# A new instruction plan for a fused retention and mixer kernel: first operations priced by their traced lengths, more zero products, a second bank for one turn

## The chip, the cores and the metric

The kernel runs on one core of a Trainium2 chip. The core has a matrix engine (TensorE, in the profile PE, its weight loads PEld), VectorE (DVE), ScalarE (ACT), GpSimd (POOL) and SyncE (SP), which issue their instructions each in program order and wait for one another through semaphores. POOL, SP and ACT also issue DMAs. The metric is the device time of one execution in microseconds (us), the median over runs.

## The reference

Four batches, eight heads, 768 tokens, head dimension 64, all inputs float32. First a retention layer, one state per head with its own decay, then a mixer block over tokens and channels:

```
for t in range(S):
    state = gamma[None, :, None, None] * state + np.einsum('bhd,bhe->bhde', k[:, :, t], v[:, :, t])
    y[:, :, t] = scale * np.einsum('bhd,bhde->bhe', q[:, :, t], state)
...
xt = x.transpose(0, 2, 1)
h = np.maximum(xt @ w_tok1, 0.0) @ w_tok2
u = x + h.transpose(0, 2, 1)
h2 = np.maximum(u @ w_ch1, 0.0) @ w_ch2
return (u + h2).astype(np.float32)
```

Here x is y with the heads side by side (512 channels); w_tok1 is 768 x 256, w_tok2 256 x 768, w_ch1 512 x 1536, w_ch2 1536 x 512.

## The kernel before

**Front** (L293 to L549), once per batch b and pair of heads p, so sixteen times. The 768 tokens are cut into six chunks of 128. In order of data:
- the loads of k, q and v (L270), issued by POOL as casting DMAs to float16, only the very first k (in the list HARD, L141) by SP in float32;
- the scaling of k by its decay, one step per head (`decayed`, L316), on VectorE or ScalarE; q is scaled either behind its turn, by one VectorE step (L356), or ahead of it (L316);
- the turn of k and of q (`turn`, L332): six or twelve TensorE transpositions into a bank of PSUM and a copy or scaling out of it (L361, L356), or, for batches 2 and 3, a transposing DMA issued by SP (L336). The list TURNS (L135) says which;
- k by v per chunk (L377), a chain of five prefix steps on VectorE (L387, L389), and its copy for both heads (L398, L401);
- the scores k by q (L417), four mask steps per pair on VectorE (L427), the products with v (L438) and with the prefix states (L447), the copy x (L453);
- the two token products (L467, L487) with a relu between (L476), the copies u and X (L493, L503), and the turn of u for the channel product (L533 and the copy L540, or a transposing DMA, L517).

**Back** (L551), once per batch: the wide product with w_ch1 (L571 for batches 0 and 1; L644, with seven products for eight, for batches 2 and 3), its relu (L587, L661, L682, L690), the narrow product with w_ch2, also with seven products for eight (L785, L795, with sums L749, copies L775 and additions L802), and the stores (L832), issued by SP or ACT. L875 and L888 make the sums of weights that the seven products need.

**What sets the order.** Front and back only make a list of 1,239 steps (`Op`, L22), each with one or more ways: an engine, an assumed cost in ns, and a function that emits its instructions. A planner, which isn't part of this file, has searched an order, an engine for each step and a bank of PSUM for each tile, from these costs; its answer is the string PLAN (L40), which `placed` (L72) decodes. In it two characters name a step, a digit the way where a step has several, a digit the bank where it opens one, and "+n" stands for n zero products: matmuls of a zero tile with 384 columns into a bank of their own (L906), which compute nothing of use. The main loop (L901) emits the steps in this order, so the string is the program order on every engine and in every DMA queue. The costs in the file have no other effect on the program.

A tile of k, q or v has four buffers; a load takes the one that came free first, and POOL, in order, holds all later loads while it waits for it. The first loads, which wait for none, follow each other in POOL's queue.

Of the kernel before, what the change touches and what calls it, by code (L numbers as in the profile page):

```python
# [9 lines left out]
F16 = mybir.dt.float16  # L10
# [11 lines left out]
class Op:  # L22
# [15 lines left out]
DIGITS = "0123456789abcdefghijklmnopqrstuvwxyzABCDEFGHIJKLMNOPQRSTUVWXYZ"  # L38

PLAN = (  # L40
    "0b07040f000d0c010g05021h1031i10e+d1n21j0060a1l41o1k009+12v61p1q1r0i1m0h082w1R02r1+11u412s10j+42t51s1x0l1v311S1"
    "0k1z1T02u01V11w1W1y1U0+21X024451Y0m1Z1t0261A11D31B1E+125421C020310272921+32x2283202y2z223352A356363402a42F500n"
    "2B0p0q+12d62I2C2301F00r0o2b2e2c02E252J2H+11G01H0s2G2D01I02N52O2K22L2f00z3f702M01J3i1K01M1L03j0u2g73701N1380v2h"
    "393a1O01P32P02i03H11Q00t2j2k02m3b3I3D13c2Q72l02R3E13n13e042n02S13d02p33h2T2W3F42U00y3g3k02X03l3o2V04f73m02o12q"
    "12Z33p00x3G12Y03004g3q64b13r3Q75240Aah34c13U3s03t3R0w0E3u03w3S3x0ae64J13z44d53v03B3T3A13J73C1ai3y03Y23K0B4K10C"
    "af3LaO4aP4e03M3NaR54L13O4h0ag4M14i3P1aj4jaSaQaU6aVaT4kaX3an43V54l3Z3WaoaWaYak63X04P1ap4004m410alaL40D42aM4314n"
    "14QamaC7aD19aI6aN4R47aEaJaZ0HaK1d44bf34501e4Sbgat44601aauaz7aAaw6axaB1caF5aGav4T0Iay5h14U4N7bhaH4o0164aq31bbi5"
    "4O4s5i0bjbkar0F4qb074pb345j1480as4rbob44ab14904W25034w65k04t1b51fbp0K4u4xb64b7b24v0bc7500G4Ybl3bd4V0bm4Z4z04y0"
    "bu5bq4X1516bn17b8bs3185425Q0be4A514524B0b97babvbt04C530bbbK0L4FbLbN4D05R0bw4E055570bz7bxbM4G0bO54H0bP15n65601g"
    "5W1bAby05o5p58bB5XbT5T05q5YbD5Z5905r5a6061bC05l05U05sbU05b05dbr0M5c05m5VbGbXbY0bEbH0J5u1047620bF5yca66r15e0c2c"  # L50
    "c75w5x6o0c6bV45S5t0bQ3c7cb04Icd5C0bW5D5f06p05v6s0c85gcf5z2cg05A5B0bR0S5E0c9bZcj6q5F7ck00P6tc0c3631354ce5GbSco6"
    "65H0bI1c165646u55I5J05Lch367cp6v5M0ci687695N06b46c5O16a0cl0O6d0c516wc410N5K15P16e66xcm6fcT2cs36y6g06zct6B05616"
    "D6Ccu6h0R6k6E6i0cUcN3cE56j06l1cVbJ1cFcv6cG6A16Fd526W1cwcO6G0cn7u0d25cP6m17v10Q6J1d3d46X0cQ36Kd6cRcx6Z1cSd77x16"
    "Hdb5dcdd7A47266I07Bcy3dw5cz700cr16ncH2d877C7y073cI7D0T74dxd9cAcJ756L1cW3cX76dydacK2cLdk7cM77dl7E7800V7FcZ6d06M"
    "5cYde2cB46Y6N0Wd1dfdmdq3dn6cCdr7G1dodgcDdp6O1dsdt5821dh7dC8A171dudv7zdidz6djdDdA8B1dG5dF8316S793724dEdBdY850dN"
    "6dH1dL7w7a7ddM00Y6P6Q06T06U07cdOe246R07be0dR8C8D0dP7H0173e31dSdQ0cq18617J7h67e27KdU7L8E07f7I7g00X7ie97eadZ7P37"
    "j07k10U7M07ldV7m07Qe17N107O07R1edee7n7q7S512dT8878G17o07p0847T7r1137U089dI2e7877V8H7s08I8a8J8b8KdJeo58cek8Le80"
    "8del7Yem8f71628F8i7W0eb8hep08e07Z06V110Zetev68g8j800eu07X0e479b07t81ec0dKewen8N0132ez9808Qe5exeA8k78n38O8R8l8P"
    "8M08oegey1eK2eq68m08p08q1ef8reGe6eh9G0eC9c0eL8s0eBeD9H08S0er8V18t8w9908TeHeY414eM6eE18W8u08v0f05eNeZf2f19aeI9J"
    "09M69e78U0eO9N8X08Y58Z9f9If38x09Oes9gf5ePeR9h9P9009i9QeJeQ5f6eS9j948y0eT91eWeX9R9dff7fa9k1ei1fgf43eU920f7950fb"  # L60
    "eVfh6fjft2f8fkfufv5fm930fxfifnfcfyfl6f9fw9l0453fA9K1fofB9nfrfsfpfK4fFej19pfqfLfG9ofefY3fM69mg07fNg42fdfZg2g196"
    "0dW1fHfOfz59q6fC9rfI8zg3g5gc9t1fPfR9u9s0fQ7g69w0g79v1fSgafTgbfDfWeF0fX9xfUgF3fE9y0gdgG0g8fVgBfJ9z9A0gj5gk0h149"
    "B09Cg99D09LgCgKgegDgE9E0gfgL09S0gggM79T6021h20gOgNgogp09F9UgH69X9V9Y19WghgQa10gI9Za2gP097a00gTgsgRa30a46gUgt0a"
    "5a60hn2gXgq7gYa7giaaa80h36gSgZgl3gJh0gxh6ab0a90h4grgugmac0gyh71gngvgwhB0hohjh86adhkhah9hp1hChD5hqhrhFhb0hEhshc"
    "gA1huhmhdhGhIhfhJhlhH3ht5hvhNhzi67hPh5hehwhghxhyic4hAhKhS2i7hOhQiahTi81hU0hWibidgV0iD5i9hXip6iehZiihVifhLikiB0"
    "hMiggW1i0hRihi4iCin1iEhY3iFiji1ioit7iqiGiriPi2i3iIisimiH6iuiW5iJiliviKiNiLi5iwiQiMizixiyiOji3dX1iAiRjE0iSiY4iU"
    "iTiX0jejk7j1jgj32j20jp1jfjF0hh0jhjj0j5j4j7iZjqiVjlj0jnj60jaj8gz0jmj9jAjBjtjbjo0jrjChi0jG7js0jJjc1jujL4jvjHjDjw"
    "jMjK0jxjQjIjy0jNjO0jRjPjW0jSjTjUjd1jV0jz1jX1jY0"
)


# [24 lines left out]
def kernel(  # L96
# [196 lines left out]
    def front(b, p):  # L293
        first, last = b == 0, b == 0 and p == NP - 1
        FA = "first" if first else "front"
        n = [0]

        def op(ways, deps=(), takes=(), uses=(), behind=None, tiled=""):
            n[0] += 1
            pe = ways[0][0] == "PE"  # L300
            pr = (-10, 0, b, n[0], p) if first else (PLACE[b, p], 0, b, p, n[0])
            return Op(ops, pr, ways, deps, takes, uses, guard=200 if pe and not first else 0, behind=behind,
                      tiled=tiled)
# [12 lines left out]
        def decayed(tag, src, dep, g, hard):  # L316
            dst, got = Slot(tag), []
            for j in range(2):
                def emit(e, j=j):
                    t, h = opened(dst, [P, NC, 2, D], F16)[:, :, j], 2 * p + j  # L320
                    if e == "ACT":
                        nc.scalar.activation(t, src.tile[:, j], AF.Copy, scale=g[:, h:h + 1])
                    else:
                        (nc.vector if e == "DVE" else nc.gpsimd).tensor_scalar(t, src.tile[:, j], g[:, h:h + 1], None,
                                                                               ALU.mult)
# [187 lines left out]
        if TURN[b, p, "u"] == "x":  # L513
            def emit():
                if UT.tile is None:
                    tile_of(UT, [P, NP, S], F16)
                nc.sync.dma_start_transpose(out=UT.tile[:, p].rearrange("d (c t) -> d c t", t=P),  # L517
                                            in_=U16.tile.rearrange(flat))
            e = Op(ops, (PLACE[b, p], 0, b, p, 99), [("SP", 1200, 1200, emit)], casts,
                   [UT] if opens else [], [U16] if opens else [U16, UT], dma=(48, 19),  # L520
                   behind=None if opens else first_of[b, "uT"])
            uT_done[b, p, 0] = uT_done[b, p, 1] = e
            if opens:
                first_of[b, "uT"] = e
        else:
            T, t = Slot(FA), None
            for lot in ([0], [1]) if last else ([0, 1],):
                c0, c1 = lot[0] * HC, lot[-1] * HC + HC

                def emit(c0=c0, c1=c1):  # L530
                    tp = T.tile if c0 else tile_of(T, [P, 1024], F16)
                    for c in range(c0, c1):
                        nc.tensor.transpose(tp[:, c * P:(c + 1) * P], U16.tile[:, c], ident16)  # L533
                t = op(one("PE", (57 * (c1 - c0), 57 * (c1 - c0) + 160), emit), [casts[x] for x in lot] + [t],
                       [] if c0 else [T], [U16, T] if c0 else [U16])

                def emit(e, c0=c0, c1=c1):
                    if UT.tile is None:
                        tile_of(UT, [P, NP, S], F16)
                    (nc.scalar.copy if e == "ACT" else nc.vector.tensor_copy)(UT.tile[:, p, c0 * P:c1 * P],  # L540
                                                                             T.tile[:, c0 * P:c1 * P])
# [397 lines left out]
```

## Time and profile before

| | us |
|---|---|
| median of 3 runs | 189.02 |
| lowest and highest | 188.54, 189.88 |
| the profiled execution | 189.19 |
| its span, first to last instruction | 187.4 |
| TensorE busy | 179.3 |
| VectorE busy | 162.2 |
| ScalarE busy | 124.0 |
| zero products (27) | 8.8 |

The profile is of one execution. Its page gives the busy time per engine and in 40 slices of the span; other views give groups of instructions by line, the chain of work that ended last, waits, single instructions in order of time, and busy time in chosen stages. In such rows "x12" is a count, "bank<-uT,wc" output and inputs by the program's names, and a bracket tells how long the engine sat idle ahead of the group and what ended it. A DMA's row has the time that its issue took; "to landing" is from the issue to the arrival of its last byte.

### The profile page before, as it was taken

To read this page: it belongs to the slowest core of one execution; us is meant where nothing else is said; L and a number is where in the kernel's file an instruction comes from. 1 tells how busy PE (TensorE), PEld (TensorE's weight loads), DVE (VectorE), ACT (ScalarE), POOL (GpSimd) and SP (SyncE) were. 2 spreads that over 40 slices of the span, in tenths; PEclk is the share of its full clock that TensorE was granted. 3 is DMA by queue.
4 is the path that set the end of the run, shared out by engine and by line. 5 is a ranking of instruction groups with operands and counts; after the bars stand their busy time and mean duration, and the time that the engine had idled before them with its cause. 6 is when DMAs were issued, how large, how long until landed. Compare 5 with 4: busy or idle time off the path is not lost.

```text
span 187.4 us, 5214 instructions
## 1 busy us (share of the span) xinstructions
PE 179.3 (96%) x2073; PEld 135.3 (72%) x2073; DVE 162.2 (87%) x427; ACT 124.0 (66%) x289; POOL 53.4 (28%) x65
## 2 busy tenths in 40 slices
PE   7698999999999999999999999999999999999992
PEld 3355788666678888866668988865688986567881
DVE  3779889849899999895379999999999899899993
ACT  6445998757899585569776568998856434773320
POOL 8997576554224006922000840000000000000000
PEclk9969999999999999999999999999999999999998
DMA  9999999999999969999999999977214033100354
GB/s 122 153 158 196 178 175 170 199 192 206 172 165 150 97 126 97 197 245 159 156 132 163 111 158 117 139 130 212 45 56 84 3 87 126 58 0 2 130 209 171
DMA packets 94377, 25.51 MB, mean 136 GB/s; under 512 B 84368, under 2 KB 91536, under 8 KB 94352
## 3 DMA queue, kind: packets, MB, share of 16 engines
q0 software_dynamic: 67456, 13.18, 90.0%
q1 hardware_dynamic: 25600, 10.03, 28.1%
q10 hardware_dynamic: 1296, 1.97, 2.9%
q8 instruction: 16, 0.26, 0.6%
q14 instruction: 9, 0.07, 0.1%
HBM read 26.74 MB, written 6.29 MB: 176 GB/s over the span
## 4 chain that ended last, share of the span: by engine, by line
PE 76%; DVE 15%; DMA 3%; issue 2%; POOL 1%; ACT 1%; DVEq 0%; POOLq 0%
PE bank L571 17%; PE bank L785 12%; PE bank L644 12%; PE bank L795 9%; PE bank L487 6%; PE bank L467 6%; PE bank L417 4%; DVE X L802 3%; DVE hs L749 3%; DMA q<-in_q_dram 3%; PE bank L438 3%; DVE h L661 3%; PE bank L447 2%; DVE am L427 2%; PE bank L346 2%
## 5 line engine op out<-in xcount | busy, mean ns | idle before, releaser
L571 PE MATMUL bank<-uT,wc 128*128 128x384 f16 x192 | 34.9, 326 | 0.2 <-DVE uT L540 0.2
L427 DVE TENSOR_TENSOR am<-bank,mask 128x384 f16<-128x384 f32 x64 | 32.6, 550 | 2.7 <-PE bank L417 2.7
L284 POOL DMA_DIRECT2D v<-in_v_dram x16 | 16.6, 1035 | 46.3 <-DVE am L427 18.4
L587 ACT ACTIVATE h<-bank 128x384 f16<-128x384 f32 x48 | 21.7, 496 | 8.5 <-PE bank L571 8.1
L571 PEld LDWEIGHTS <-wc 128*128 128x128 f16 x192 | 17.7, 98 | 9.9
L785 PEld LDWEIGHTS <-hs 128*128 128x128 f16 x216 | 20.4, 98 | 2.9 <-DVE hs L749 0.4
L775 ACT COPY us<-bank 128x256 f32<-128x256 f32 x31 | 11.3, 376 | 16.4 <-PE bank L785 14.7
L656 ACT COPY us<-bank 128x384 f32<-128x384 f32 x36 | 16.6, 484 | 8.0 <-PE bank L644 5.0
L802 DVE TENSOR_TENSOR X<-X,bank 128x256 f32<-128x256 f32 x48 | 19.0, 416 | 1.4 <-PE bank L785 0.7
L661 DVE TENSOR_TENSOR h<-bank,us 128x384 f16<-128x384 f32 x36 | 18.8, 552 | 1.6 <-PE bank L644 1.0
L785 PE MATMUL bank<-wsum,hs 128*128 128x256 f16 x144 | 19.2, 273 | 0.0
L284 POOL DMA_DIRECT2D k<-in_k_dram x15 | 15.5, 1041 | 5.6 <-DMA wc<-in_moe_w_ch_dram 1.4
L389 DVE SCALAR_TENSOR_TENSOR U<-U,gs,bank 128x64 f32<-128x64 f32 x64 | 16.4, 277 | 0.8
L493 ACT CAST u<-bank 128x384 f16<-128x384 f32 x29 | 13.3, 482 | 5.2 <-PE bank L487 5.0
L453 ACT CAST x<-bank 128x384 f16<-128x384 f32 x29 | 13.2, 487 | 4.4 <-PE bank L447 4.3
L644 PE MATMUL bank<-hs,wsum 128*128 128x384 f16 x72 | 15.2, 326 | 0.1
L795 PEld LDWEIGHTS <-h 128*128 128x128 f16 x144 | 13.6, 97 | 2.1 <-issue 0.3
L467 PE MATMUL bank<-x,wt 128*128 128x128 f16 x192 | 14.9, 220 | 0.0
L487 PE MATMUL bank<-h,wt 128*128 128x128 f16 x192 | 14.2, 220 | 0.0
L503 ACT COPY X<-bank 128x384 f32<-128x384 f32 x29 | 13.9, 494 | 0.2 <-DVE u L493 0.2
L802 DVE TENSOR_TENSOR X<-X,us 128x256 f32<-128x256 f32 (+1 forms) x25 | 13.0, 537 | 0.2
L467 PEld LDWEIGHTS <-wt 128*128 128x128 f16 x192 | 12.0, 98 | 1.3
(85 smaller groups left out, 352.4 us busy)
## 6 DMA issues: line engine op xcount, KB each, us to landing
out_dram<-X SPq DMA_DIRECT2D x16, 256.0 KB, 2.7
v<-in_v_dram POOLq DMA_DIRECT2D x16, 192.0 KB, 9.4
q<-in_q_dram POOLq DMA_DIRECT2D x16, 192.0 KB, 10.6
k<-in_k_dram POOLq DMA_DIRECT2D x15, 192.0 KB, 10.0
wc<-in_moe_w_ch_dram POOLq DMA_DIRECT2D x5, 512.0 KB, 12.7
out_dram<-X ACTq DMA_DIRECT2D x6, 256.0 KB, 2.2
wt<-in_moe_w_tok_dram POOLq DMA_DIRECT2D x2, 384.0 KB, 8.7
wc<-in_moe_w_ch_dram POOLq DMA_DIRECT2D x2, 256.0 KB, 10.4
```

The lines of the kernel that those rows point to most:

```text
L284: (nc.sync if hard else nc.gpsimd).dma_start(out=s.tile, in_=src.rearrange("h (c p) d -> p h c d", p=P))
L427: nc.vector.tensor_tensor(am, SC[g].tile[:, :m * P].rearrange("p (i t) -> p i t", t=P), mask.to_broadcast([P, m, P]), ALU.mult)
L467: nc.tensor.matmul(acc[:, jt * P:(jt + 1) * P], wt1[:, i, jt * P:(jt + 1) * P], X16.tile[:, i], start=(i + jt == 0), stop=(i == NC - 1), s ...
L487: nc.tensor.matmul(Y[hf].tile[:, i * P:(i + 1) * P], wt2[:, jt, t], H1.tile[:, jt], start=False, stop=(jt == NJ - 1), skip_group_check=True)
L571: nc.tensor.matmul(acc[:, :SH], wc1[:, ct, ft * P:(ft + 1) * P], UT.tile[:, ct, sh * SH:(sh + 1) * SH], start=(ct == 0), stop=(ct == NP - 1))
L587: nc.scalar.activation(H2.tile[:, ft], A.tile[:, :SH], AF.Relu)
L644: nc.tensor.matmul(acc[:, :SH], left(ct), r[:, ct], start=first and ct == 0, stop=ct == 1, skip_group_check=True)
L656: (nc.scalar.copy if e == "ACT" else nc.vector.tensor_copy)(kept(j), A.tile[:, :SH])
L661: nc.vector.tensor_tensor(into(hf)[:, ft], bank.tile[:, :SH], kept(j), ALU.add)
L785: nc.tensor.matmul(acc_[:, lo], l[:, j], r[:, j], start=first and j == 0, stop=j == K2 - 1, skip_group_check=True)
L795: nc.tensor.matmul(acc_[:, lo], l[:, j], r[:, j], start=first and j == 0, stop=j == K2 - 1, skip_group_check=True)
L802: (nc.vector if e == "DVE" else nc.gpsimd).tensor_tensor(dst(), dst(), b_(), ALU.add)
```

## The change

Three things are edited. In `decayed` the assumed cost of a VectorE scaling of the very first k goes from (335, 420) to (800, 900) ns. The turn of u in batch 0, last pair, which is made in two halves (`last`), gets a bank for each half. And PLAN is another string.

```diff
-    "0b07040f000d0c010g05021h1031i10e+d1n21j0060a1l41o1k009+12v61p1q1r0i1m0h082w1R02r1+11u412s10j+42t51s1x0l1v311S1"
...
+    "0405070f0b0001021h10d0a030e1i1+i1j4061l01k01m0g081R01n51o0c091p1V11S01q1v46+81T21W1u101y1r1U01z1s1w+42v21x0i2r"
...
-                got.append(op(either(emit, ACT=(506, 610), DVE=(335, 420) if hard else (232, 312)),
+                got.append(op(either(emit, ACT=(506, 610), DVE=(800, 900) if hard else (232, 312)),
...
-            T, t = Slot(FA), None
+            t = None
             for lot in ([0], [1]) if last else ([0, 1],):
                 c0, c1 = lot[0] * HC, lot[-1] * HC + HC
-
-                def emit(c0=c0, c1=c1):
-                    tp = T.tile if c0 else tile_of(T, [P, 1024], F16)
+                T = Slot(FA)
+
+                def emit(c0=c0, c1=c1, T=T):
+                    tp = tile_of(T, [P, 1024], F16)
                     for c in range(c0, c1):
-                        nc.tensor.transpose(tp[:, c * P:(c + 1) * P], U16.tile[:, c], ident16)
+                        nc.tensor.transpose(tp[:, (c - c0) * P:(c - c0 + 1) * P], U16.tile[:, c], ident16)
...
-                                                                             T.tile[:, c0 * P:c1 * P])
+                                                                             T.tile[:, :(c1 - c0) * P])
```

Decoded, both strings hold the same 1,239 steps. 64 of them change engine: 28 from VectorE to ScalarE, 22 the other way, 14 between SP and ACT as issuers of stores. The zero products go from 27 (13, 1, 1, 4, 2, 1, 3, 1, 1 in order) to 39 (18, 8, 4, 3, 2, 1, 3). The beginnings, with q02 for the q of batch 0, pair 2:

| queue | before | after |
|---|---|---|
| POOL | v00 q00 q02 k02 k01 q01 v01 k03, a constant, v02 q03, token weights 1 and 2, v03 q10 k10 q11 | v00 q00 q01 k01 k02, the constant, q02 v01 q03, token weights 1, v02 k03, token weights 2, v03 k10 q10 q12 |
| TensorE | 13 zero, k by v 00, turns k00 q00, 1 zero, turn q02, 1 zero, half the scores 00, 4 zero, turn k02, other half, turns k01 q01, 2 zero, k by v 01, half the scores 01 | 18 zero, turns k00 q00, k by v 00, turn q01, half the scores 00, 8 zero, turn k01, other half, 4 zero, turn q02, half the scores 01, 00 by v (one half), 3 zero, k by v 01, other half |
| VectorE, from the end of the first k on | four prefix steps and the mask, q00, q02, k02 (two), prefix, mask step 00, k01, three mask steps (q01 between), prefix steps and masks of 01, then q03 | q00, three prefix steps and the mask, q01, mask steps and prefix steps of 00 in turn, q02, masks and prefix steps of 01, q03, masks of 02 |
| ScalarE, from its first copy on | copy k00, half of k01, copies k02 k01 | copy k00, both halves of k01, copy k01, both of k02 |

Further on, SP's queue changes too. Around the scores of batch 2, pair 2, it held before: store, k22 and q22 turned, q23, k23; after: a store, q22, q30, k22, a store, k23, k30 (each a transposing DMA). The loads that POOL holds back until a v of batch 1, pair 3 is done with are before v22 k22 q23 q22 k30 q30 k31 q31 v31; after v23 k23 k22 q30 q22 k30 q31 q33 k31. The stores of batch 0 stand later in the new string than in the old one.

More of the change, by code (lines that the diff above doesn't have):

```diff
@@ L46 @@
[L46 to L65, printed above, removed]
@@ new lines @@
+    "q2J0p2y3102b2z3202E322A2G2B2e+33331J1M2c02f02C3413f132H2D01K11L01N02g73i1O02h3763j2K12N02O382i02L3e232j392m3D0"
+    "3E12M03a2P03h3b0w3g2k03F72Q32l02n02R2o02S03k23c3G10s3n51P63d12p72W3l1Q00r2T4b13o3H32q10o2U13m04N62V04f43p03q74"
+    "c10u3r2X02Y04O2Z13s03003I4d63t3w4g0v3Q07313U3u00t3v0ah43T3z24e03R3J14h64i0Aae34j3K0z3x03A03S0xaf4k3Lai3y00E3B0"
+    "an5ak74lagal0G3Maj3N3C0ao3O4m3P1am4J1aX3apaO4aPaU63Y0aVaR5aQ3V2aYaWb66aZ1d3W3X0az7b7aS1bb84K00yaT3Zb04b1aAb240"
+    "0bf3bg4L11faL5aBaM4M14175h042aNbh5i1194n0aF65l14314W34750H1a5m4Z4450aG474P14QaH5j7450aI6aJ4604R4Xat54Y481au5k0"
@@ new lines @@
+    "aKaw74904S4Tax5Q04o3260b944U4r0C0Day0B4s541aC74paDbaaq6aravaE4V1513bc54w01eas0Fbdbi6bb4q5R0b34be4t252bo5304u4v"
+    "04xbl7bmbq554y0bj4a4z5bp4Abnb41g1c4B0bu7bO515bk4C4Fbs65600I164D0b5bv1757718bK4E0bLbt0585n25W45X4G0590bxbP05obz"
+    "70Kby05a5T05b05Y4I0L5U1bBbwbT0ObC06r05Z4H05pbU0bA5qbD5rbr605d6s05s61bGbE5c00M6205e0bM5u0274bHbV35y5Vcc6c65xbWc"
+    "dca45t05vbXbZ5C65w0JbQ7bN5S6o05f05z25g5Acb1c0c7bFc85D0SbR6p06u0cfbY06v6wc2c96x6t5B05E0cg05F3c30Pcj6y5G6zch70N5"
+    "H0ci6335010V0Q5I5Lck0clco5J05M066655K064675N0cm5O56806b26q69cp6B41636F6C6E5P06ccK76a0cLcs5dh36d0ctd24cudidn6d3"
@@ new lines @@
+    "0TcN5cOd4do6e40YcM14dj6fdpc1cPcZ7cE6cF6W1cB5cCcG6g1850d06Z16A16h6Ddk6861d1cW3c40bJ16i1cDcX6k6G7dlcY6J1cy4cQ570"
+    "1cncRcz6l16j06X0717u1dm6m0cSdq3cA6Hd866K820d96I07v1bSdb5cv2cwdr87dacH46L1dc0W726ds7A0cx736M2cT3dd6YcU746N7BcVc"
+    "Id55d6c517C757wcJd78316O1dw26PdxdC76dt56Q06R0e440R7D7E84777F8A1cq1dDdudye5dv7906326S7x0dI77d6T00Ude27c780df8D0"
+    "6n7y1dz3dEdJ7b6U07adAdFdG4dgdBdN6ekdO7h17i7e3ce8E07zel882dH0898a7f8b7g0dL0X7j0dM0dR7k58c8d7ldS8B0en7m0dP7H6502"
+    "7nem7Kev7139J07JdQ07IdUeq57q0Z7Lew7M2dV7o06V8F8e0dY7G0e26er7P0e07r07Q7N8G57s09K0dZez7p08C980e318H7O08Ie77R08Je"
@@ new lines @@
+    "947S3eA7T7U0e81ebdT8K8Leaec0991118f7351e17V8i8g7Y8h8jed8M0eo7eedKbI17W07Z0800egef7X0ep09G08k2cr08N13048let8m0e"
+    "h8P8Oeu08n58o10eK38Q9H08R129e6818p0ex9f9b09c18q0ey08S1eL8r8T9geC9heY48s08V09i8weB8W8U09jes9k0eGeD8t9M78X08Y6e6"
+    "8u08x07t8v18ZeZ8y0eH9Nf02900eO9af2eP9OeM59deI9Pf46eR9QeN91f39ReSf1f59IeJ9S0eQ7eW8zfh294f6eTeX920ff5f7eUfg950fa"
+    "eVft3f8fbdW1961ei1f9dX1fv7fufi930fjg44fxfkfefy9l1260fwej0fmfAfM79o9nfl6fdeE1fnfrfBfFfofK2fsfLfpfG9m9pfqfY59q1f"
+    "ZfNfOfcfPfH9t09ufz39r9s0g2g06fCfR9LfIg3fDg1g5fQ7fSgcg69w69v1fWfXfTgag79xfEgdgbgBfUg8fVgC9y0g9gF59C9T2673gG0gKg"
@@ L69 @@
+    "Njbj0jz0jO0gW1jc1jd0jQjPjTjW1jRjSjUjX0jV1jY1"
 )
```

17 lines of the change are left out of this document (8 added, 9 removed).

## The prediction

> **What bounds the kernel now.** I read the page first, then the busy time by stages, then the chain, then single loads and transposing DMAs. The stages (columns: stage, length, busy time and count of PE, PEld, DVE, ACT, POOL, granted clock, DMA share, GB/s):
>
> ```profile
> span 187.4 us, 5214 instructions
> 5.50:8.90 3.40, 1.86 (x33) 1.14 (x35) 2.40 (x7) 1.15 (x2) 3.40 (x5) 1.00 1.73 154
> 8.90:12.30 3.40, 3.40 (x29) 1.97 (x29) 2.91 (x7) 0.61 (x1) 3.28 (x7) 0.50 1.99 159
> 12.30:15.70 3.40, 2.85 (x58) 2.02 (x57) 2.71 (x6) 2.42 (x4) 3.24 (x5) 1.00 2.16 164
> 15.70:19.10 3.40, 3.00 (x53) 2.09 (x50) 3.37 (x12) 2.23 (x5) 2.40 (x3) 1.00 1.36 206
> 35.00:152.00 117.00, 116.99 (x1394) 90.41 (x1393) 103.66 (x264) 86.10 (x207) 25.93 (x26) 1.00 1.34 138
> 152.00:183.60 31.60, 31.37 (x242) 23.05 (x240) 29.70 (x71) 13.56 (x33) 0.00 (x0) 1.00 0.25 89
> 183.60:187.40 3.80, 0.20 (x2) 0.00 (x0) 0.68 (x3) 0.00 (x0) 0.00 (x0) 0.87 0.58 198
> ```
>
> TensorE is idle for 0.01 us of the 117 from 35 to 152, and for 0.23 of the next 31.6. The change removes no product of use there, so these 149 us can only stay or grow. The last 3.8 us are the last additions and stores. What an order can save lies ahead of 35: there VectorE is nearly full (3.37 of 3.40 in 15.7 to 19.1), and TensorE waits for it or for loads. The chain of that stretch (start, length, what), with the spacings that I use below:
>
> ```profile
> 3.40 5.37 DMA q<-in_q_dram
> 8.81 0.80 PE bank L346 x12
> 10.48 1.39 PE bank L906 x4
> 14.93 0.47 DVE am L427
> 18.25 0.67 DVE U L389 x3
> 18.92 0.87 DVE qT L356
> 34.33 0.37 DVE uT L540
> 34.74 0.32 PE bank L571
> 44.15 3.25 PE bank L571 x20
> 61.57 1.31 PE bank L785 x12
> ```
>
> A mask step holds VectorE for 0.47 us, a prefix step 0.2, a scaled q 0.87; a matmul of 384 columns takes 0.163, of 256 0.109.
>
> **The change, part by part.** *The price in the planner* (800 for 335 per half of the first k) emits nothing: 0 us by itself. The first scaling runs as before, since its load and its constant come as before.
>
> *The first 35 us.* New loading order: q01 and k01 ahead of q02 and k02, q03 and the first token weights ahead of v02 and k03. The loads land one behind the other, so a load takes the landing time of the place that it moves to (issue rows, and landing after the issue, in us):
>
> ```profile
> 5.39 0.96 DVE L324 TENSOR_SCALAR k<-us,gk 128x384 f16<-128x384 f32 x1
> 8.46 0.96 DVE L356 TENSOR_TENSOR qT<-bank,gq 128x768 f16<-128x768 f16 x1 [0.49 <-PE bank L346]
> 4.11 1.05 POOL L284 DMA_DIRECT2D k<-in_k_dram  x1
> k<-in_k_dram POOLq DMA_DIRECT2D x1, 192.0 KB, 5.9
> 7.83 1.07 POOL L284 DMA_DIRECT2D k<-in_k_dram  x1
> k<-in_k_dram POOLq DMA_DIRECT2D x1, 192.0 KB, 7.2
> 10.44 0.72 POOL L278 DMA_DIRECT2D q<-in_q_dram  x1
> q<-in_q_dram POOLq DMA_DIRECT2D x1, 192.0 KB, 6.6
> 11.13 0.86 POOL L260 DMA_DIRECT2D wt<-in_moe_w_tok_dram  x1
> wt<-in_moe_w_tok_dram POOLq DMA_DIRECT2D x1, 384.0 KB, 8.4
> L322 ACT ACTIVATE k<-k,gk 128x384 f16<-128x384 f16 x14 | 8.5, 618 | 3.4 <-DMA k<-in_k_dram 3.4
> L361 ACT COPY kT<-bank 128x768 f16<-128x768 f16 x6 | 4.8, 814 | 2.8 <-PE bank L348 2.8
> ```
>
> By hand: both kernels end the first k at 6.35 (5.39 + 0.96) and start the first scaled q at 8.46. After it the new VectorE order is three prefix steps and the mask (0.7), the second q from 10.05, two mask steps and two prefix steps to 12.2. k01 lands at 10.0 (4.11 + 5.9); ScalarE scales it (2 x 0.62) to 11.2, TensorE turns it, ScalarE copies it (0.81) to 12.55. Two mask steps to 13.2, the third q to 14.1, four mask and four prefix steps (2.7) to 16.7, the fourth q to 17.6. Before, that fourth q ended at 19.8 (18.92 + 0.87): 2.2 us ahead. Part of it goes back: the token weights land about 17.0 (10.44 + 6.6) instead of 19.5 (11.13 + 8.4), but the fourth k lands about 19.4 instead of 15.0 (7.83 + 7.2), as four later places lie ahead of it; its turn is ready about 21.5 and the first two mask steps of the last pair end at 23.3, where the old plan had 23.9. From there the new order is as dense; the first matmul that needs the fourth turn of u stands at about 34.1 for 34.74, with 0.3 us more of other work behind it. Gain: 0.6 to 1.1 us, if zero products cost 0.16 each.
>
> *Twelve more zero products.* Eighteen stand first; at 0.35 each (1.39 for four in the chain) they end by 7.4, ahead of the first q, which VectorE has at 8.46 after its turn: nothing. Eight stand between the first scores and the turn of k01, from 9.9: at 0.16 they end at 11.2, just when k01 is scaled; at 0.35 they end at 12.5, and the scores behind them come 1.1 to 1.3 late: VectorE, which I counted as full, then waits. Which it is hangs on the granted clock: 3.40 us with TensorE busy for 1.86 were followed by 0.50, those with 2.85 and 3.00 by 1.00. For the new order I count in 5.5 to 8.9 zero products 0.8, turn of k 0.5, first q 0.5, k by v 0.35, start of the second q 0.1: 2.25, between the rows and a little nearer to 1.86. So the gain is 1.1 or about 0; I take 0.6.
>
> [...]
>
> *Two banks for the last turn of u.* Both halves went through one bank; the copy of the first half started at 34.33. With a bank each it need not follow the second transposition. It is worth less than the 0.37 us that one such copy takes, and is contained in the above.
>
> *35 us and on, order searched anew.* Nothing to win but 0.24. What can be lost is a transposed operand that is late. SP issues these in order, and how long they take depends on the loads that run beside them:
>
> ```profile
> 63.17 1.21 SPq L336 DMA_TRANSPOSE qT<-q  x1
> qT<-q SPq DMA_TRANSPOSE x1, 2.8
> 71.74 1.01 POOL L284 DMA_DIRECT2D v<-in_v_dram  x1 [12.64 <-DVE X L802]
> 85.36 1.22 SPq L336 DMA_TRANSPOSE kT<-k  x1
> kT<-k SPq DMA_TRANSPOSE x1, 7.8
> 87.76 4.05 SPq L336 DMA_TRANSPOSE qT<-q  x2
> qT<-q SPq DMA_TRANSPOSE x1, 8.9
> 89.14 2.67 SPq L336 DMA_TRANSPOSE qT<-q  x1
> qT<-q SPq DMA_TRANSPOSE x1, 10.0
> 98.09 0.51 PE L417 MATMUL bank<-qT,kT 64*128 64x128 f16 x12
> ```
>
> A quiet queue gives 2.8; while the nine loads run that POOL lets go from 71.74 on, it is 7.8 to 10.0. The scores of batch 2, pair 2 (98.09) had both operands at 96.7 (87.76 + 8.9). In the old plan 10.5 us of TensorE work stand between the second half of that q and these scores, and k went ahead of q. In the new plan 9.0 stand there (40 matmuls of 384 columns 6.5, 6 of 256 0.65, the rest 1.85), and SP issues q of that pair, then a q of batch 3 that isn't needed for 20 us, then k. So k is issued 0.4 + 2 x 1.24 = 2.9 us after the q is scaled, and lands 2.8 to 10.0 later: 5.7 to 12.9 against 9.2 with the change of mode at the scores. The stall is 0 to 3.7. The same loads stand in the same place (a v of batch 1 lets them go, 14 us of TensorE work ahead of that q in both plans), so I go by the loaded rows: 7.8 gives 1.5, 8.9 gives 2.6, and of the two I take 2.2, a bit above the middle, since the two DMAs ahead of it share the queue. TensorE takes its work in order: all behind these scores waits with them. Stalls elsewhere: +0.1, of 0 to 1: batch 1 and the first wide product need their loads earlier than in the old order.
>
> *Steps that change engine.* 28 go from VectorE to ScalarE and 22 back, 14 stores and issues change between ScalarE's and SP's queues. From 35 on neither VectorE (103.66 of 117) nor ScalarE (86.10) sets the end: 0, with a part of the stalls above as the price where a step comes late. POOL's constant goes ahead of the third q: nothing, since loads land 5 us and more behind their issue.
>
> *The end.* The last three stores go from ScalarE's queue to SP's: +0.1, of 0 to 0.2.
>
> **Sum.** The profiled execution took 189.19 (span 187.4 and 1.8 around it), 0.17 above the median of 189.02. 189.19 - 0.6 + 2.2 + 0.1 + 0.1 = 191.0; less 0.17 it is 190.8.
>
> **Rivals.** *The transposed k is in time* (a quiet queue, 2.8, or fewer stores beside the loads): no stall, 189.02 - 0.6 + 0.2 = 188.6. For it: the new plan stores batch 0 later than the old one, so fewer bytes run beside the loads. Against it: all transposing rows from 81 to 92 stand at 7.8 or above.
> *The clock halves and that DMA is in time*: the zero products do nothing, 189.2.
> *The start gives more*: the 2.2 us at the fourth q stay and nothing stalls, 189.02 - 2.2 + 0.1 = 186.9. Against it: the fourth k lands 4.4 later than before.
> *The loaded queue takes its longest time*: 10.0 for that k (3.7 us of stall), and the q of batch 2, pair 3, which has 5.5 us of TensorE work between its scaling and its scores, needs 0.4 + 7.8 and adds 2.5: 189.02 - 0.6 + 6.2 + 0.2 = 194.8. It decides from a landing time of 6.3 on (9.2 - 2.9).
>
> **How the numbers follow.** The forecast, 190.8, has a chance of 0.45 and a range of its own of 189.7 to 191.9; the k in time 0.23; the halved clock 0.08; more at the start 0.10; the longest time 0.14. About 1% (1.9 us) is what a measurement of this kernel can tell from no change. Faster by over 1% is the 0.10 and 0.02 of the k in time; slower the 0.14 and, as 190.9 lies in the forecast's middle, 0.21 of its 0.45: 0.35; the same 0.53. From 187.9 to 193.0 lie all but the third rival and most of the fourth.
>
> **What would show it.** Right: TensorE busy for all but a little of 35 to 90, then one gap of 1.5 to 2.6 us ahead of scores (L417) near 95 to 99, laid to a DMA of kT; the fourth scaled q ending near 17.6 to 18.7; a granted clock of 0.50 or 1.00 in the window behind 8.9 with the gain at the start to match. Wrong: no gap there and a span of 185 to 187; or gaps at the wide product of batch 0 (weights late) or behind 104, which I priced at 0.1.

## The result and the profile after

| | us |
|---|---|
| changed kernel, median of 4 runs (191.28 to 191.63) | 191.38 |
| kernel before, beside it, 4 runs (188.54 to 189.88) | 189.09 |
| ratio, with its 95% interval | 1.012 (1.0082 to 1.0158) |
| the profiled execution of the changed kernel, and its span | 191.63, 189.9 |

The change makes the kernel 1.2% slower. 190.8 was forecast. Where the runs of a kernel lie further apart, a ratio leaves out those over 1.5% above its fastest. In the changed file the lines behind the edit have moved by one (L571 is now L572, L785 is L786, L832 is L833).

The page of the changed kernel, span, busy time and the shares of the chain that ended last:

```profile
span 189.9 us, 5246 instructions
PE 180.3 (95%) x2085; PEld 136.4 (72%) x2085; DVE 161.3 (85%) x421; ACT 127.4 (67%) x296; POOL 53.5 (28%) x65
PE 57%; DVE 19%; DMA 9%; ACT 6%; POOL 4%; issue 2%; DVEq 0%; ACTq 0%; POOLq 0%
PE bank L572 11%; PE bank L645 10%; PE bank L786 10%; PE bank L796 7%; DVE X L803 6%; DMA kT<-k 5%; DVE hs L750 4%; DMA wt<-in_moe_w_tok_dram 4%; PE bank L467 4%; PE bank L487 4%; PE bank L417 2%; PE bank L438 2%; PE bank L447 2%; DVE h L662 2%; DVE am L427 2%
```

The same two rows of the chain, of the kernel before:

```profile
PE 76%; DVE 15%; DMA 3%; issue 2%; POOL 1%; ACT 1%; DVEq 0%; POOLq 0%
PE bank L571 17%; PE bank L785 12%; PE bank L644 12%; PE bank L795 9%; PE bank L487 6%; PE bank L467 6%; PE bank L417 4%; DVE X L802 3%; DVE hs L749 3%; DMA q<-in_q_dram 3%; PE bank L438 3%; DVE h L661 3%; PE bank L447 2%; DVE am L427 2%; PE bank L346 2%
```

A DMA of kT now holds 5% of the chain, where the kernel before shows none. The stages say where (columns as before: stage, length, busy time and count of PE, PEld, DVE, ACT, POOL, granted clock, DMA share, GB/s):

```profile
5.50:8.90 3.40, 2.96 (x51) 2.03 (x49) 1.99 (x5) 1.23 (x2) 3.28 (x7) 1.00 1.76 158
8.90:12.30 3.40, 2.95 (x30) 1.55 (x26) 3.24 (x10) 1.91 (x4) 3.40 (x5) 1.00 2.03 173
35.00:95.00 60.00, 59.89 (x692) 44.96 (x691) 48.29 (x123) 44.75 (x106) 21.69 (x22) 1.00 1.77 153
95.00:106.00 11.00, 9.29 (x122) 7.27 (x119) 8.44 (x24) 7.99 (x20) 2.02 (x2) 1.00 1.44 189
106.00:150.00 44.00, 43.72 (x517) 34.45 (x517) 42.03 (x107) 31.86 (x78) 2.02 (x2) 1.00 0.69 111
```

The last two of them in the kernel before:

```profile
95.00:106.00 11.00, 11.00 (x145) 9.11 (x143) 10.25 (x26) 7.08 (x18) 2.31 (x3) 1.00 1.15 125
106.00:150.00 44.00, 43.99 (x530) 35.01 (x528) 42.50 (x110) 33.40 (x83) 3.74 (x4) 1.00 0.89 108
```

The clock stays at 1.00 behind 8.9, where the kernel before had 0.50. TensorE is idle for 1.71 us of 95 to 106, and for 0.28 of the 44 us behind; in the kernel before it is idle for none of the 11 and 0.01 of the 44. The gap, as SP issued and as TensorE met it (issues with landing times behind the issue, then the matmul row with what it waited for):

```profile
85.15 2.66 SPq L336 DMA_TRANSPOSE qT<-q  x2
87.90 1.45 SPq L336 DMA_TRANSPOSE kT<-k  x1
qT<-q SPq DMA_TRANSPOSE x1, 8.0
kT<-k SPq DMA_TRANSPOSE x1, 9.5
97.45 0.51 PE L417 MATMUL bank<-qT,kT 64*128 64x128 f16 x12 [1.63 <-DMA kT<-k]
```

SP issues the q of the pair, the q of batch 3, and only at 87.90 the k, which lands at 97.4 (87.90 + 9.5); the scores stand at 97.45, idle for 1.63 before.

An idle bracket doesn't show a matmul that comes late without a gap long enough to be listed. So I counted for each run how far TensorE is behind its own work: the products in the plan's order, each at its spacing when nothing waits (0.163 us per 384 columns and so on, zero products at 0), are added up, and the sum is taken from the time at which each starts. In this lag a step is a loss, a flat stretch none. Between two orders at the same sum it is only as good as the spacings of the small products: with slightly other ones it moves by up to 0.3. At the last product, where all work is done, nothing of that is left. Here at 70, 90, 100 and 160 us of work, with the last product and the span (us; the rows below the second are runs told below):

| run | 70 | 90 | 100 | 160 | last product | span |
|---|---|---|---|---|---|---|
| before | 19.25 | 19.65 | 20.08 | 21.76 | 183.53 | 187.4 |
| changed | 18.21 | 20.82 | 21.36 | 23.83 | 185.61 | 189.9 |
| changed, again | 18.69 | 20.58 | 21.12 | 23.61 | 185.39 | 189.6 |
| end queues | 18.23 | 20.51 | 21.05 | 23.55 | 185.32 | 189.3 |
| k ahead | 19.04 | 20.34 | 20.88 | 23.33 | 185.11 | 189.4 |
| k ahead, old rest | 18.01 | 20.81 | 22.02 | 23.55 | 185.33 | 189.2 |
| old, 18 zeros | 18.46 | 18.87 | 19.30 | 20.95 | 182.73 | 186.9 |
| old, two banks | 18.74 | 19.15 | 19.58 | 21.27 | 183.05 | 187.2 |
| new start, k and v early | 18.99 | 19.39 | 19.83 | 21.49 | 183.27 | 187.5 |

Against before, the changed kernel is 1.04 ahead at 70, loses 2.61 where before loses 0.40 (the scores, 70 to 90), and from 90 on 3.01 against 2.11. At the last product it is 2.08 behind (185.61 - 183.53), and behind that stand 4.3 us against 3.9.

### The profile page after: what moved, and what is told of

Read it like the earlier page. It is cut to its first block, busy times and chain, and to the rows that moved or that the text cites. A ratio compares the mean times of both kernels' runs of the same rounds, so it can differ in the third digit from the quotient of the medians.

```text
span 189.9 us, 5246 instructions
## 1 busy us (share of the span) xinstructions
PE 180.3 (95%) x2085; PEld 136.4 (72%) x2085; DVE 161.3 (85%) x421; ACT 127.4 (67%) x296; POOL 53.5 (28%) x65
## 4 chain that ended last, share of the span: by engine, by line
PE 57%; DVE 19%; DMA 9%; ACT 6%; POOL 4%; issue 2%; DVEq 0%; ACTq 0%; POOLq 0%
PE bank L572 11%; PE bank L645 10%; PE bank L786 10%; PE bank L796 7%; DVE X L803 6%; DMA kT<-k 5%; DVE hs L750 4%; DMA wt<-in_moe_w_tok_dram 4%; PE bank L467 4%; PE bank L487 4%; PE bank L417 2%; PE bank L438 2%; PE bank L447 2%; DVE h L662 2%; DVE am L427 2%
## 5 line engine op out<-in xcount | busy, mean ns | idle before, releaser
L572 PE MATMUL bank<-uT,wc 128*128 128x384 f16 x192 | 36.0, 326 | 0.1
L776 ACT COPY us<-bank 128x256 f32<-128x256 f32 x33 | 12.3, 378 | 21.2 <-PE bank L786 21.1
L572 PEld LDWEIGHTS <-wc 128*128 128x128 f16 x192 | 17.4, 98 | 9.1 <-issue 0.3
L786 PEld LDWEIGHTS <-hs 128*128 128x128 f16 x216 | 20.4, 98 | 3.0 <-DVE hs L750 0.6
L786 PE MATMUL bank<-wsum,hs 128*128 128x256 f16 x144 | 19.5, 273 | 0.1
L493 ACT CAST u<-bank 128x384 f16<-128x384 f32 x26 | 12.3, 488 | 4.2 <-PE bank L487 3.2
L487 PE MATMUL bank<-h,wt 128*128 128x128 f16 x192 | 14.8, 219 | 0.0
L467 PE MATMUL bank<-x,wt 128*128 128x128 f16 x192 | 14.4, 219 | 0.4 <-DMA wt<-in_moe_w_tok_dram 0.4
```

The lines of the kernel that those rows point to most:

```text
L467: nc.tensor.matmul(acc[:, jt * P:(jt + 1) * P], wt1[:, i, jt * P:(jt + 1) * P], X16.tile[:, i], start=(i + jt == 0), stop=(i == NC - 1), s ...
L487: nc.tensor.matmul(Y[hf].tile[:, i * P:(i + 1) * P], wt2[:, jt, t], H1.tile[:, jt], start=False, stop=(jt == NJ - 1), skip_group_check=True)
L572: nc.tensor.matmul(acc[:, :SH], wc1[:, ct, ft * P:(ft + 1) * P], UT.tile[:, ct, sh * SH:(sh + 1) * SH], start=(ct == 0), stop=(ct == NP - 1))
L786: nc.tensor.matmul(acc_[:, lo], l[:, j], r[:, j], start=first and j == 0, stop=j == K2 - 1, skip_group_check=True)
```

## The experiments

Each runs beside the kernel before on its chip (medians 189.06 to 189.23 there). My theory: the time is lost where k is late in SP's queue, and in the newly searched order behind. Rivals: the load burst makes k late whatever SP's order; the start is worth something else than I think.

### The changed kernel once more

Unedited.

> The changed kernel once more, unedited, as the yardstick for the runs beside it, since its first 24 us came out 0.85 us later in the run with k ahead than in its first profile. Theory (the start of the new plan differs from execution to execution: the moment at which the granted clock goes to 1.00 and the landing of the loads differ): the single times spread over more than 0.8 us, the median lies between 191.3 and 192.0, and the gap of 1.6 to 1.9 us at the scores of batch 2, pair 2 is there in any case. Rival (the start is the same each time, and the run with k ahead lost 0.85 by its edit): the times lie within 0.4 of 191.4.

191.50 (191.07 to 192.15, 6 runs), ratio 1.0123 (1.0096 to 1.0149). The times spread by 1.1, the lag at 70 is 0.48 larger than in the first profile, and the scores' gap is there, but of 0.9 us: it was expected at 1.6 to 1.9 in any case. A TensorE that comes later waits less for the same k. So a profile's start can't be taken for the kernel's: over the old plan's start at 70 I have 19.25, 18.46, 18.74 and 19.34 (the last from the run with k late), mean 18.95; over the new one 18.21, 18.69, 18.23, 19.04, 18.01 and 18.53 (the last from the run with the old plan's rest), mean 18.45. The new start gains 0.5 us on average, not the 1.04 of one pair of profiles. The single values of a start spread by 0.8 to 1.0, and two of the four old starts carry an edit of their own (18 zeros, two banks), so this mean is good to about 0.5.

### k ahead of the q of batch 3

Step 432, `6Y`, goes in front of step 503, `87`:

```diff
-...wv2cwdr87dacH46L1dc0W726ds7A0cx736M2cT3dd6YcU746N7BcVc
+...wv2cwdr6Y87dacH46L1dc0W726ds7A0cx736M2cT3ddcU746N7BcVc
```

> The changed kernel with one step moved in the plan: the transposing DMA of k of batch 2, pair 2 goes on SP's queue ahead of the one of q of batch 3 instead of behind it. In the changed kernel it is issued at 87.9 us, lands 9.5 later, and TensorE stands for 1.8 us at those scores. Theory (the place in SP's queue decides): k takes the landing of the DMA whose place it gets, 1.3 to 2.9 us earlier, the gap of 1.8 shrinks to between 0 and 0.5, and the time falls by 1.3 to 1.8, to about 189.8. Rival (the burst of loads decides, whatever the order on SP): k lands at 97.4 again, the gap stays at 1.8, and the time stays at 191.4. Second rival (something else is late right behind): the gap goes, another opens within 10 us, and the time falls by less than 0.8.

191.18 (190.61 to 192.82), ratio 1.0114 (1.0085 to 1.0143): by the time alone not told from the changed kernel. The trace tells more. SP's issue, its landing, TensorE at these scores and at those of the next pair, the issue and landing of the q of that next pair, and the stage:

```profile
87.45 1.33 SPq L336 DMA_TRANSPOSE kT<-k  x1
kT<-k SPq DMA_TRANSPOSE x1, 8.1
96.59 0.51 PE L417 MATMUL bank<-qT,kT 64*128 64x128 f16 x12
105.04 0.51 PE L417 MATMUL bank<-qT,kT 64*128 64x128 f16 x12 [0.59 <-DVE hs L750]
99.40 1.21 SPq L336 DMA_TRANSPOSE qT<-q  x1
qT<-q SPq DMA_TRANSPOSE x1, 5.5
95.00:106.00 11.00, 10.41 (x134) 8.33 (x132) 10.00 (x29) 8.83 (x21) 2.02 (x2) 1.00 1.40 180
```

k lands at 95.55, 1.9 earlier although this run's start was 0.83 later, and the scores follow without a gap: the place in the queue decides, and the rival of the burst falls. But the second rival holds too: the next scores, of pair 3, wait at 105.04. The profile names hs for it, a step of VectorE that ended at 105.00; but these scores neither read it nor take a bank that it holds. They need the q of pair 3, which SP issues at 99.40 and which lands at 104.90 (99.40 + 5.5), and the kernel before has issued it at 89.14. In the changed kernel it lands at 103.42, and the scores that were late before it hid it. The busy time of VectorE, 10.00 of 11 us, isn't the cause: the kernel before has 10.25 in the same 11 us, and TensorE waits for nothing. From 70 to 90 the loss is 1.30 instead of 1.89 to 2.61, still 0.9 above the old order's 0.40. The late k costs 0.6 to 1.3 by itself; of the rest of that loss, 0.59 is the wait for this q, which stood hidden behind it. In the median times, 0.2 to 0.3 of the late k arrives.

### The old kernel with that k behind two q

```diff
-5cYde2cB46Y6N0Wd1df...8A171dudv7zdidz6djdD...
+5cYde2cB46N0Wd1df...8A171dudv7z6Ydidz6djdD...
```

(`6Y` moves from in front of `6N` to behind step 469, `7z`.)

> The old kernel with one step moved: the transposing DMA of k of batch 2, pair 2 goes on SP's queue behind the q of that pair and of the next, instead of ahead of them. In the old kernel the last of the three was issued at 89.1 and landed 10.0 later, at 99.1; the scores stand at 98.1. Theory (the place in SP's queue decides): k lands at 98.8 to 100.5, a gap of 0.7 to 2.4 us opens ahead of those scores, and the time rises by as much, to 189.9 to 191.6. Rival (the order on SP doesn't matter there, the queues share the work): no gap over 0.3 and 189.2.

194.38 (192.46 to 196.15), 5.3 above the kernel before: more than twice the most that was expected. SP's issues, two waits of TensorE and the stages behind them (of its profiled execution, at 196.15 the slowest of the six, span 194.3):

```profile
87.86 2.62 SPq L336 DMA_TRANSPOSE qT<-q  x2
90.53 6.10 SPq L336 DMA_TRANSPOSE kT<-k  x2
100.30 0.51 PE L417 MATMUL bank<-qT,kT 64*128 64x128 f16 x12 [2.04 <-DMA kT<-k]
102.59 1.46 PE L795 MATMUL bank<-wsum,hs 128*128 128x256 f16 x6 [1.78 <-DVE hs L749]
101.20:107.90 6.70, 5.31 (x29) 3.94 (x30) 5.21 (x13) 2.26 (x6) 0.00 (x0) 0.50 0.42 99
108.00:115.00 7.00, 7.00 (x127) 6.26 (x126) 6.11 (x15) 3.50 (x9) 4.66 (x5) 1.00 1.05 91
```

The wait for k is 2.04, inside what was expected. But behind the scores VectorE has its steps still to do (1.78 more), and from 101.20 to 107.90 the granted clock is 0.50: the six products at 102.59 take 1.46 where six take 0.82 at 1.00 (k ahead, 102.31). The lag grows by 7.0 from 70 to 90, 2.04 + 1.78 of it waits. The one run with a mean clock of 1.00 took 192.46, 3.4 above the kernel before: about the two waits alone. One DMA in the wrong place costs its wait, what stood behind it, and, in this execution, 6.70 us at half the clock.

### The new order up to the scores, the old one behind

The plan as it is for 671 steps, and the steps left over in the old order, with the old engines and banks; once with the late k, once with k ahead:

```diff
 <the first 671 steps of the new plan>
-<the rest of the new plan>
+<the steps left over, as the old plan has them>
```

> The new plan up to the scores of batch 2, pair 2 (its first 671 steps, to about 99 us), with the late k as it is, and behind it the remaining steps in the order, on the engines and with the banks of the old plan. Theory (the order behind 99 us loses 1.3 us by gaps of 0.2 to 0.5 and 0.4 at the end, all of its own): the gap of 1.8 stays, those gaps go, and the time falls by 1.2 to 1.7 from the changed kernel's, to about 189.9. Rival (they come from what the late scores pushed back, whatever the order): the time stays within 0.4 of the changed kernel's.

> The two edits together: the k of batch 2, pair 2 ahead of the q of batch 3 on SP's queue, and the old plan's rest behind the scores of that pair. Theory (the two losses are separate, 1.3 to 1.9 and 1.2 to 1.7): both go, and what is left is the new start: the time falls by 2.6 to 3.4 from the changed kernel's, to 188.0 to 188.8, below the old kernel's 189.2. Rival (VectorE, with 10.0 us busy of the 11 from 95 to 106 when k is ahead, is the next bound, and gives back 0.7 or more as it did at the scores of batch 2, pair 3): 188.8 to 189.5, no faster than the old kernel.

193.30 (192.07 to 194.08), ratio 1.0212 (1.0175 to 1.0249), and 190.82 (190.51 to 191.26), ratio 1.0084 (1.0059 to 1.0108). Both miss: the first is slower than the changed kernel, the second gains 0.7 of the 2.6 to 3.4 expected. A seam breaks them. The row with k ahead, just behind it:

```profile
102.01 0.81 PE L786 MATMUL bank<-wsum,hs 128*128 128x256 f16 x6 [2.22 <-DVE us L776]
115.00:150.00 35.00, 34.62 (x398) 26.80 (x396) 33.46 (x84) 27.45 (x68) 0.00 (x0) 1.00 0.67 96
```

In that trace VectorE works without a gap from 96.9 to 102.7, and the products that the old rest brings next wait for it; the new order has done other steps by then than the old one had at the same scores. What can be read is behind the seam: from 100 to 160 us of work the lag grows by 1.53 (22.02 to 23.55), in the kernel before by 1.68, in the changed one by 2.47. The new order loses 0.8 to 0.9 there by itself; the old rest, pushed back by nearly 2 us, doesn't. And with k ahead in the new order, where those scores come without a gap, the loss is 2.45, as in the changed kernel. The rival, that those small losses come from what was pushed back, falls.

### The clock and the zero products

Eighteen zero products for thirteen in the old plan (`+d` becomes `+i`), and thirteen for eighteen in the new one (`+i` becomes `+d`).

> The old kernel with 18 zero products at the start instead of 13, and nothing else. Theory of the clock: the busy time in 5.5 to 8.9 rises from 1.86 to about 3.1, the clock behind 8.9 is 1.00 instead of 0.50, and TensorE gains part of the 1.7 us that the half clock costs there; VectorE with 2.91 busy of 3.40 in that window lets no more than about 0.5 of it through: the time falls by 0.2 to 1.0, to about 188.5. Rival (VectorE and the loads set the start, not the clock): the clock is 1.00 and the time stays at 189.1. Second rival (the clock doesn't hang on busy time before it): 0.50 again and 189.1.

> The changed kernel with 13 zero products at the start, as the old one has, instead of 18; all else is the new plan. The start of the new plan gained 1.05 us on TensorE's work, with a granted clock of 1.00 behind 8.9 us where the old kernel showed 0.50. Theory (the five extra zero products fill the window of 5.5 to 8.9, and so keep the clock): without them that window's busy time falls from 2.96 to 1.6 to 1.9, the next shows a clock of 0.50, TensorE falls back by 0.4 to 1.1 us, and the time rises to 191.8 to 192.5. Rival (the new order's own products fill the window well enough): the clock stays at 1.00, and the time stays within 0.2 of 191.4.

The old kernel with 18: 189.08 (188.66 to 190.04, 12 runs), ratio 0.9997 (0.9982 to 1.0011). The stages of its start:

```profile
5.50:8.90 3.40, 3.03 (x47) 1.84 (x45) 2.81 (x7) 1.15 (x2) 3.40 (x5) 1.00 1.67 158
8.90:12.30 3.40, 2.34 (x25) 1.18 (x25) 3.30 (x7) 0.84 (x2) 3.28 (x7) 1.00 2.05 163
```

Filled to 3.03, the window is followed by 1.00, as expected, and the time hardly moves: the rival holds so far as the clock doesn't set this start. That VectorE (3.30 of 3.40) and the loads do is likely, and not tested. Among the 66 runs of the kernel before, the 24 with a mean clock under 0.99 have a median of 189.34, the 31 with 0.995 and more 189.06: the half clock costs that start about 0.3 by these medians.

The new kernel with 13: 192.13, of 190.74 to 194.16, ratio 1.0124 (1.0096 to 1.0151). Its profiled execution took 194.08, with one other of 194.16 the slowest of the six; there a turn of q takes 0.85 for 0.53 in the changed kernel, which is the second row:

```profile
7.84 0.85 PE L346 MATMUL bank<-ident,q 128*64 128x128 f16 x12 [0.60 <-DMA q<-in_q_dram]
```

```profile
7.12 0.53 PE L346 MATMUL bank<-ident,q 128*64 128x128 f16 x12
```

In that trace eight zero products at 10.25 take 2.74, in the changed kernel eight at 9.04 take 1.48; only the four at 13.98 take 0.82, as four do in the changed kernel at 11.68. In the changed kernel the first record of 1.00 begins at 6.49, and with k ahead a turn of q at 7.75 takes 0.53. So without the five products this start stayed slow up to 13.98 in that execution. What they are worth in time is not shown: the ten runs of the changed kernel's two lots stayed within 191.07 to 192.15, but the ratio here is the changed kernel's own, and k ahead, which has all eighteen, has a run of 192.82. Neither the theory nor its rival is settled by this.

### Two banks alone

Step 223 of the old plan, `3B`, becomes `3B0`, and the edit of the turn comes with it.

> The old kernel and its old order, with the two-bank edit alone: the second half of the last turn of u in batch 0 takes bank 0 of its own, instead of the other half of the first one's bank. Theory (it frees one copy of 0.37 us from a wait, beside a chain that VectorE and the weights set): 0 to 0.15 us, 189.0 to 189.1. Rival (the copy stands in the chain, at 34.3, and TensorE's wait behind it goes): 188.7.

188.83 (188.44 to 189.45, 12 runs), ratio 0.998 (0.9961 to 0.9998). I can't lay this to the banks: from 8 to 20 us of work, where the turn stands, its lag grows by 1.91, in the kernel before by 1.81, and its profile's start came 0.6 earlier, which the edit doesn't touch. Eleven of its 12 runs had a mean clock of 0.99 or more, with a median of 188.74; the 14 such runs of the kernel before beside it had 188.85. So compared, the edit is worth 0 to a tenth.

### The queues at the end

The last four stores on the queues of the old plan (`jW1`, `jV1`, `jY1` to 0, `jX0` to 1):

> The changed kernel with the last four stores on the queues that the old plan gives them: three on ScalarE's, one on SP's, instead of the other way round. Theory (SP issues four stores one behind the other at the end, 3.2 us of issues, and the last lands later): the time between the last product and the end goes from 4.3 us back to 3.9, and the time falls by 0.2 to 0.5, to about 191.1. Rival (the end is set by the last additions, in the new order 0.4 later behind the last product): the span behind the last product stays at 4.2 or above and the time at 191.4.

191.10 (190.92 to 191.14, 5 runs), ratio 1.0101 (1.0077 to 1.0124), 0.3 to 0.4 below the changed kernel's medians, which were taken on other chips; the intervals of the ratios overlap. Behind the last product stand 4.0 us (189.3 - 185.32) for 4.3; but the kernels with the old plan's end give 3.9 to 4.2 as well (table), so the gain of these queues is likely and not sure. SP's issues at the end, changed kernel first:

```profile
183.64 3.19 SPq L833 DMA_DIRECT2D out_dram<-X  x4
```

```profile
183.36 2.67 SPq L833 DMA_DIRECT2D out_dram<-X  x2
```

### The new start on the old body

The new plan for 233 steps, then the old one; then with v of batch 1, pair 2 earlier among the loads (`0y` behind `0t`), then with k of that pair earlier too (`0z` in front of `0t`).

> The new plan for its first 233 steps (to about 38 us; loads, start, zero products, the two banks), and the rest of the steps in the order, on the engines and with the banks of the old plan. Theory (the start gains 1.05 us and all that is lost is lost in the order behind it): the gain stands to the end, since TensorE is busy throughout, and the time is 189.1 - 1.05 = 188.0, with no gap over 0.5 us behind 40 us. Rival (loads and transposing DMAs of the old body come at their own times, and a TensorE that runs 1 us ahead only waits for them): the gain is given back by 100 us, 189.1.

> The new start and the old plan's rest again, with one load moved: v of batch 1, pair 2 goes to the 26th place of POOL's order, which the old plan gives it, instead of the 31st, which the new one does. With it late, TensorE waited 2.7 us for it at 43 us, and half a clock behind that cost the rest of 4.2. Theory (the losses of the new kernel lie in what was ordered anew behind the start, and the new start is a gain where the loads fit the body): that gap goes, no other opens, TensorE ends 0.3 to 1.0 ahead of the old kernel, and the time is 188.2 to 188.9 against 189.1. Rival (the gain at the start has no way through the old body: the next load or VectorE is late in its place): 189.1 or above, with a new gap behind 35 us.

> As the run with v of batch 1, pair 2 earlier, and k of that pair earlier too: k goes to the 22nd place of POOL's order, ahead of the second column block of the channel weights, and v behind that block. In the run before, k was issued at 28.0, landed 10.4 us later, and its scaling held TensorE up for 1.1 us at 39; the old plan issues it at 20.1. Theory (a start that runs ahead is a gain where the loads of batch 1 fit the body behind it): issued about 4 us earlier, k lands by 35, no gap over 0.5 is left behind 30 us, TensorE ends 0.3 to 1.0 ahead of the old kernel, and the time is 188.2 to 188.8. Rival (the queue is full there, and what k and v gain the weights of the wide product lose): another gap of 0.5 to 1.5 between 34 and 45, and 189.2 to 190.0.

192.64 (191.88 to 193.64), ratio 1.0188 (1.0159 to 1.0218); 190.01 (189.61 to 192.79), ratio 1.0052 (1.0035 to 1.007); 189.24 (188.76 to 190.01, 12 runs), ratio 1.0006 (0.9982 to 1.0031). The first was expected at 188.0. The gap in it and the stage behind, then the gap in the second, TensorE and the scaling that it waits for:

```profile
43.34 0.35 PE L377 MATMUL bank<-v,k 128*64 128x64 f16 x10 [2.71 <-DMA v<-in_v_dram]
44.60:47.90 3.30, 3.30 (x19) 1.92 (x17) 2.94 (x8) 1.36 (x3) 1.30 (x2) 0.50 1.25 207
```

```profile
39.09 0.51 PE L348 MATMUL bank<-ident,k 128*128 128x128 f16 x6 [0.97 <-DVE k L324]
38.48 0.55 DVE L324 TENSOR_SCALAR k<-k,gk 128x384 f16<-128x384 f16 x2 [0.93 <-DMA k<-in_k_dram]
```

Each load moved ahead took its gap away, and none over 0.5 is left in the third. Yet that is 189.24 and not the 188.2 to 188.8 expected: its lag at 70 is 18.99, level with the old starts' mean of 18.95. At 20 us of work it is still 0.8 ahead of the kernel before, at 25 only 0.4. What takes the difference are short waits around the place where the two plans are joined, at 38 us, such as this one:

```profile
39.57 0.34 PE L438 MATMUL bank<-v,am 128*128 128x64 f16 x6 [0.25 <-ACT h L588]
```

So the gain is gone although the loads are back in their places; whether the new start or the join costs it, no run tells apart. No version here beats the kernel before by more than 0.2%, and the one that does by so much owes it to no edit that I can name.

## Why the prediction came out as it did

Two of its terms were right, one was oversized, and one far too small; the errors offset each other in part, so that 190.8 came within 0.6 of the time by some luck.

- *The start* (-0.6, of 0 to -1.1). Right on average, 0.5; in the profiled execution 1.04, at the end of the range that I gave to a clock that stays at 1.00. It did, and 5.5 to 8.9 was filled to 2.96, where I had counted 2.25: the last 13 of the eighteen zero products take 4.15 us from 2.70 on, 0.32 each, and reach to 6.85, and of them alone 1.35 lie in it. My own 7.4 for their end would have given 1.9; the 0.8 that I counted doesn't agree with it. And 5.50 to 8.91 was a record of the clock in the old profile only; in the new one the first record begins at 6.49, and the 3.41 us from there on happen to be as full, 2.97. The fourth scaled q ended at 17.58, as worked out (17.6). But my reason was wrong by half: the old start doesn't gain by a full clock more than 0.3.
- *The scores of batch 2, pair 2* (+2.2). The place, the queue and the cause were right, and moving that one DMA shows it from both sides. The size came out by two errors that offset each other: the k took 9.5 to land, longer than the 7.8 and 8.9 that I weighed, but from the end of the scaling of q (85.09) TensorE had 10.7 us of work up to these scores (95.82), where I counted 9.2. Of that sum 0.2, my estimate, were for the change of mode at the scores (tiles of 128x128 to 64x128); with k ahead, where nothing waits, the scores start 0.09 behind the products before them (96.59 for 96.17 + 2 x 0.163). The gap is 0.9 to 1.6, as the k lands at 97.2 to 97.4 whenever TensorE arrives; with what follows, 70 to 90 us of work cost 1.5 to 2.2 more than before, of which 0.9 stays when k is in time. I put all of it on the k; where that is in time, most of what stays (0.59) is the wait for the q of pair 3, also a transposing DMA, which my last rival had named with 2.5.
- *Stalls elsewhere* (+0.1, of 0 to 1). This step failed: 0.9 from 90 us of work on, at the top of its bounds. I had thought of late loads, and none of the losses is one: they are short waits of TensorE, mostly for what VectorE frees or makes, such as this one, which is listed with 0.15 but sets the product back by 0.3:

```profile
124.26 0.48 PE L645 MATMUL bank<-uT,wc 128*128 128x384 f16 x2 [0.15 <-DVE X L503]
```

- *Steps that change engine* (0). I argued that with 103.66 busy of 117 VectorE sets nothing. Its busy time is indeed not what changed: from 106 to 150 it is 42.03 of 44 us, in the kernel before 42.50, where TensorE loses nothing. What I left out is the order of VectorE's steps: TensorE waits where the step that it needs stands behind others in VectorE's program order. It is the cause of the step above that failed. Which of the moved steps cost the 0.9 stays open.
- *The end* (+0.1). 0.2 to 0.4: 4.2 to 4.3 us behind the last product against 3.9 to 4.2; with the stores on the old queues 4.0. That is within what traces of one end differ by.
- *The sum*: -0.5 + 1.9 + 0.9 + 0.2 = 2.5 by the traces, 2.3 to 2.4 by the medians (191.38 - 189.09, 191.50 - 189.06); forecast 1.8.
- *The rivals*: the k in time (188.6) didn't come, and when I made it so, the trace gained 0.6 to 1.3 of the 2.2 that I had priced, the median time 0.2 to 0.3. Of more at the start (186.9) the fourth scaled q is there, 2.2 ahead (17.58 for 19.79), but TensorE's work came out only 0.5 ahead on average. The clock didn't halve. Of the longest time (194.8) the landing of the k came near, 9.5 for 10.0, but TensorE's longer work took half of it away, and the q of pair 3 landed in time.

## What to carry to other kernels

When an order is searched anew, look in the new one for every transposed operand whose DMA stands behind one that isn't needed for long, and price its wait with the landing times of the loaded queue (here 7.8 to 10.0 us, where one DMA on a quiet queue took 2.8). Then do the same for the next one behind it: a wait that is mended uncovers the next late operand, here 8.5 us further on. Check the name that a profile gives a wait against what the instruction reads and overwrites: here it named a step that ended 0.1 us after the landing that mattered. And ask, step by step, what stands ahead of the steps that TensorE needs in VectorE's order: late ones made many small losses here, 0.9 us in all, that no single row shows, and the share of busy time doesn't tell, since VectorE was as busy (42.50 of 44 us for 42.03) where TensorE waited for nothing. Compare starts over several traces: here the same instructions came out up to 1 us apart.

## What the hardware showed

The trace of the kernel before has a record of the granted clock of 3.41 us at 1.00 from 5.50 on, one of 3.41 at 0.50 from 8.91, one of 174.08 at 1.00 from 12.33, and 0.50 from 186.40 to the end. That of the changed kernel has one, 1.00 from 6.49 to the end. Ahead of the first record products are slow: the 18 zero products of the changed kernel take 5.72 from 1.12 on, 0.32 each, and the 13 of the kernel before 4.34, 0.33 each, where 384 columns take 0.163 later. With 13 zero products in the new plan they were slow up to 13.98. The stage 8.90 to 12.30 of that run is printed with 1.00 all the same, so the length of the products tells there what the printed clock doesn't.

In front of a 0.50 stood, in the kernel before, 3.40 us with TensorE busy for 1.86 (5.5 to 8.9); in the new start on the old body 3.90 us with 1.19 (40.6 to 44.5), 2.71 idle in one piece; in the old kernel with k late 6.10 us with 3.76 (95 to 101.1), 2.04 idle, with 1.78 more behind the scores. In front of a 1.00 stood 2.96 and 3.03 of 3.40 (5.5 to 8.9, changed kernel and old with 18 zeros), and 2.34 of 3.40 (8.9 to 12.3, the latter).

An idle stretch at the scores of batch 2, pair 2 of 0.90, 1.29 and 1.63 us (changed again, end queues, changed) was followed by six products in 0.82, the length at 1.00. With the old rest behind the scores a gap of 2.22 us left it at 1.00 in the run with k ahead (95 to 106, six products in 0.81); the same gap, with the late k, was followed by six products in 1.24, in an execution with a mean clock of 0.991. How much of this goes by the busy time, by the length of a gap or by its place, no run here separates. In the old kernel with k late, the lag grew by 7.0 over waits of 3.82 (2.04 + 1.78); 6.70 us at 0.50 are worth 3.35 by my estimate, about the rest.
